# Eight attention jobs with places of their own, v scaled by ScalarE, tails issued by ScalarE, and weights rounded one chunk at a time

## The chip, the cores and the metric

One core of a Trainium2 chip. Times are device microseconds (us) of one execution, medians of several. All runs compared here are beside runs of the kernel before on the same chip.

## The reference, cut to what matters

```python
B, H, S, D = 8, 8, 576, 64
scores = 1/sqrt(D) * q @ k.T
Dmat[h, i, j] = gamma[h] ** (i - j) if i >= j else 0     # retention: decay per head
attn = (scores * Dmat) @ v                               # (B, H, S, D)
x = attn.transpose(0, 2, 1, 3).reshape(4608, 512)        # tokens x d_model
xn = x / sqrt(mean(x * x) + 1e-6) * rms_g
out = (silu(xn @ w_gate) * (xn @ w_val)) @ w_out         # d_ff = 1536; the weights are float64
```

The kernel splits the attention into 32 *jobs* of two heads. The float64 weights come in 18 *chunks* of 1 MB, which are rounded to float32 on chip: an *exponent* step (one VectorE operation, then three on ScalarE), a *mantissa* of three VectorE operations, and a *join* (one). Before the first projection can run, eight jobs must be done and the first two chunks rounded. This beginning is all that the change touches.

## The kernel before

A job's transposes; each result goes to a PSUM bank of a pool of five, and ScalarE copies it out. `last` of `turn` holds the tails (the last 64 rows of q and k):

```python
    def turn(j):
        d = st[j]
        hp = jobs[j][1]
        last = bank(f"turn_{j}_t")
        for nm in "qk":
            ps = bank(f"turn_{j}_{nm}")
            ...                                    # TensorE: four blocks of q or k into ps
            nc.scalar.copy(out=t[:, : NFULL * P], in_=ps)
        for i, nm in enumerate("qk"):
            ...                                    # TensorE: the tail into last[:, o]
            nc.scalar.copy(out=d[nm + "T"][:, NFULL * P :], in_=last[:, o])
        for e in range(2):                         # scale v by the decay, on GpSimd
            for t in (d["v"][:, :, e], d["vt"][:, e].unsqueeze(1)):
                g = gv[: t.shape[0], hp, e : e + 1].unsqueeze(2).to_broadcast(list(t.shape))
                nc.gpsimd.tensor_tensor(out=t, in0=t, in1=g, op=ALU.mult)
```

The states of a job (TensorE) end in a bank of the same pool, `d["last"] = bank(f"last_{j}")`; VectorE reads it in the last of the job's running sums. The order of the rounding, and the beginning:

```python
    def rounding():
        exponent(0); yield
        exponent(1); yield
        yield from mantissa(0); yield
        for i in range(len(chunks)):
            if i + 1 < len(chunks):
                yield from mantissa(i + 1); yield
            join(i)
            n_chunks += 1
            load_chunks(i + 4)
            yield
            if i + 2 < len(chunks):
                exponent(i + 2); yield
    ...
        load_first(0); load_tails(0); load_first(1); load_first(2)       # all by the sync queue
        load_chunks(1, nc.sync)
        for i in (1, 0, 2, 3):
            table(i)                                                     # issued by ScalarE
        nc.scalar.dma_start(out=rms_g, in_=...)
        turn(0)
        for j in range(8):
            slot(j)                         # values of j-1, scores, states, sums of j, carried of j-1
            if j + 1 < 8:
                turn(j + 1)
            ...                             # part of the norm of unit 0
            if 1 <= j <= 5:
                load_first(j + 2)           # waits for a buffer of k and v
            if j == 1:
                load_tails(1)
            ...
            load_chunks((1, 2, 2, 3, 3, 4, 4, 4)[j], nc.sync)
            weights((0, 1, 2, 2, 2, 2, 1, 0)[j])                         # rounding steps
```

## Time and profile before

| kernel before | |
|---|---|
| time | 1186.49 us, median of 3 (1185.11 to 1187.63) |
| span of the profiled run | 1186.8 us (one more execution, of 1188.96 us) |
| TensorE, VectorE, ScalarE, GpSimd busy | 97%, 57%, 20%, 5% (62.0 us) |
| rounds of the first eight jobs | 8.63, 5.77, 6.23, 6.61, 11.79, 10.07, 8.38, 7.95 us |
| first up matmul; start of its steady stretch | 69.37; 90.35 us |

A *round* runs from one job's first transposing matmul to the next job's. From 90.35 us on TensorE hardly waits, so a kernel is faster by as much as that point comes earlier, if the rest keeps its length. The profile counts an engine's wait before the instruction that ended it and names a releaser; "issue" means that the profile shows nothing it waited for.

### The profile page before, as it was taken

The page shows a single profiled execution, that of the slowest core. Times are in us where ns is not written, and L with a number is a line of the kernel's source. Part 1 is how long each engine was busy: PE and PEld are TensorE (multiplying, and loading weights), DVE is VectorE, ACT ScalarE, POOL GpSimd, SP SyncE. Part 2 cuts the span into 40 slices and gives each one's busy share as a digit, 9 for nine tenths or more (in the row PEclk, how much of TensorE's full clock was granted, in tenths as well). Part 3 has the DMA queues.
Part 4 walks back from the last instruction along what each step waited for, and adds up shares of the span by engine and source line. Part 5 has one row for each costly group of instructions (what it writes and reads, how often), then busy time and mean ns, then how long its engine had stood idle before and what let it go on. Part 6 is the DMA issues. An engine that isn't in the chain of part 4 may idle for free.

```text
span 1186.8 us, 24268 instructions
## 1 busy us (share of the span) xinstructions
PE 1147.7 (97%) x10320; PEld 1039.1 (88%) x10320; DVE 672.2 (57%) x1362; ACT 238.9 (20%) x452; POOL 62.0 (5%) x106
## 2 busy tenths in 40 slices
PE   7679999999999999999999999999999999999998
PEld 6555555448999999999999999999999999999998
DVE  4678785027765674464675666356566555536442
ACT  4325653012111120121120211220220110120110
POOL 2300004420000000000000000000000000000000
PEclk9799999999999999999999999999999999999999
DMA  8724431422755546315525456306435412403304
GB/s 223 180 63 142 146 138 36 137 66 49 203 149 87 131 121 116 110 44 103 146 61 119 100 132 130 123 2 133 101 98 127 118 49 83 131 1 93 121 1 107
DMA packets 282219, 125.23 MB, mean 106 GB/s; under 512 B 257152, under 2 KB 264704, under 8 KB 282112
## 3 DMA queue, kind: packets, MB, share of 16 engines
q1 hardware_dynamic: 271824, 108.44, 36.9%
q10 hardware_dynamic: 10288, 15.25, 4.1%
q8 instruction: 81, 1.33, 0.5%
q14 instruction: 26, 0.21, 0.1%
HBM read 108.70 MB, written 14.94 MB: 104 GB/s over the span
## 4 chain that ended last, share of the span: by engine, by line
PE 78%; DVE 11%; ACT 5%; DMA 3%; issue 2%; SPq 1%; POOL 0%; DVEq 0%; POOLq 0%; ACTq 0%
PE x L456 13%; PE z L456 13%; PE w L456 13%; PE wo L586 7%; PE y L456 6%; PE out L527 5%; PE xo L586 4%; PE zo L586 4%; PE yo L586 3%; PE up L513 2%; DVE sum L298 2%; PE av L334 2%; ACT w_gate L708 1%; ACT w_gate L709 1%; ACT w_gate L712 1%
## 5 line engine op out<-in xcount | busy, mean ns | idle before, releaser
L480 ACT COPY m<-x 128x384 f32<-128x384 f32 x60 | 28.7, 478 | 429.7 <-PE x L456 429.7
L456 PE MATMUL z<-x,w_gate 128*128 128x192 f32 x480 | 88.2, 327 | 2.2 <-DVE sum L298 2.2
L456 PE MATMUL x<-x,w_gate 128*128 128x192 f32 x480 | 89.8, 331 | 0.0
L456 PE MATMUL x<-x,w_val 128*128 128x192 f32 x480 | 88.7, 328 | 0.0
L456 PE MATMUL w<-sums,w_gate 128*128 128x192 f32 x480 | 88.0, 327 | 0.0
L456 PE MATMUL z<-x,w_val 128*128 128x192 f32 x480 | 87.8, 326 | 0.0
L456 PE MATMUL w<-sums,w_val 128*128 128x192 f32 x480 | 87.8, 326 | 0.0
L586 PE MATMUL xo<-h,w_out 128*128 128x192 f32 x480 | 82.1, 328 | 0.0
L586 PE MATMUL wo<-h,w_out 128*128 128x192 f32 x480 | 82.0, 328 | 0.0
L456 PEld LDWEIGHTS z<-x,w_gate 128*128 128x128 f32 x480 | 79.6, 190 | 2.5 <-DVE sum L298 2.5
L456 PEld LDWEIGHTS x<-x,w_gate 128*128 128x128 f32 x480 | 80.5, 192 | 0.5
L456 PEld LDWEIGHTS w<-sums,w_gate 128*128 128x128 f32 x480 | 80.0, 191 | 0.0
L456 PEld LDWEIGHTS x<-x,w_val 128*128 128x128 f32 x480 | 79.2, 190 | 0.6
L456 PEld LDWEIGHTS w<-sums,w_val 128*128 128x128 f32 x480 | 79.7, 190 | 0.0
L456 PEld LDWEIGHTS z<-x,w_val 128*128 128x128 f32 x480 | 79.6, 190 | 0.0
L586 PEld LDWEIGHTS xo<-h,w_out 128*128 128x128 f32 x480 | 78.1, 190 | 0.5
L586 PEld LDWEIGHTS wo<-h,w_out 128*128 128x128 f32 x480 | 78.1, 190 | 0.0
L463 DVE TENSOR_TENSOR u<-m,y 128x384 f32<-128x384 f32 x60 | 32.8, 546 | 78.0 <-PE y L456 75.6
L463 DVE TENSOR_TENSOR h<-u,w 128x384 f32<-128x384 f32 x60 | 33.2, 554 | 75.0 <-PE w L456 75.0
L513 PE MATMUL up<-x,w_gate 128*128 128x384 f32 x192 | 65.2, 498 | 4.9 <-DVE w_gate L742 3.1
L475 ACT ACTIVATE h<-h 128x384 f32<-128x384 f32 x90 | 47.0, 523 | 88.8 <-DVE h L463 88.8
L513 PE MATMUL up<-x,w_val 128*128 128x384 f32 x192 | 62.7, 487 | 1.7 <-ACT w_val L521 1.7
(124 smaller groups left out, 1756.8 us busy)
## 6 DMA issues: line engine op xcount, KB each, us to landing
w_out<-w_blocks SPq DMA_DIRECT2D x70, 768.0 KB, 5.3
k<-in_k_dram SPq DMA_DIRECT2D x64, 128.0 KB, 3.1
v<-in_v_dram SPq DMA_DIRECT2D x64, 128.0 KB, 3.8
out_dram<-o SPq DMA_DIRECT2D x304, 24.0 KB, 1.6
qraw<-in_q_dram SPq DMA_DIRECT2D x96, 72.0 KB, 2.7
kraw<-in_k_dram SPq DMA_DIRECT2D x96, 72.0 KB, 2.8
w_blocks<-w_out SPq DMA_DIRECT2D x7, 768.0 KB, 6.9
w_out<-in_moe_w_gate_dram ACTq DMA_DIRECT2D x4, 1024.0 KB, 5.2
```

Source lines behind the costliest of these rows:

```text
L298: nc.vector.scalar_tensor_tensor(out=t[:, c], in0=t[:, c - 1], scalar=gc[:, hp : hp + 1], in1=part, op0=ALU.mult, op1=ALU.add,)
L334: mm = nc.tensor.matmul(av[odd][side(e), i * L : i * L + L], lhsT=d["sum"][side(e), c - 1], rhs=d["qT"][side(e), c * L : c * L + L], start ...
L456: nc.tensor.matmul(ps[:, i * HU : i * HU + HU], lhsT=w_up[m][:, 2 * blk + c, cut], rhs=t_of[u][blk][:, c], start=(start and i == c == 0), ...
L463: nc.vector.tensor_tensor(out=o, in0=a, in1=pairs_of(ps), op=ALU.add)
L475: nc.scalar.activation(out=o, in_=c, func=AF.Silu)
L480: nc.scalar.copy(out=s1, in_=pairs_of(x_))
L513: nc.tensor.matmul(ps[:, :U], lhsT=w_up[m][:, 4 * half + c, i * P : i * P + P], rhs=x_of[u][:, c], start=(c == 0), stop=(c == NHP - 1),)
L527: nc.tensor.matmul(ps[:, :DM], lhsT=h_of[u][:, f, s * P : s * P + P], rhs=w_out[:, f], start=(f == 0), stop=(f == NF - 1),)
L586: nc.tensor.matmul(ps[:, i * HU : i * HU + HU], lhsT=w_slots[:, k % 4, c, i * P : i * P + P], rhs=rhs[:, c], start=(start and i == c == 0) ...
L708: nc.scalar.activation(out=e.bitcast(F32), in_=e, func=AF.Relu, bias=least)
L709: nc.scalar.activation(out=e.bitcast(F32), in_=e.bitcast(F32), func=AF.Relu, bias=most, scale=-1.0)
L712: nc.scalar.activation(out=e, in_=e.bitcast(F32), func=AF.Relu, bias=top, scale=-(2.0**23))
```

## The change

Its intent is to take waits out of the beginning. k and v of all eight jobs get places that nothing else uses by then, so that the sync queue can issue all loads at once; ScalarE scales v, as it does in all later jobs, so that GpSimd does not disturb VectorE; the first tails are issued by ScalarE, beside the sync queue; and a chunk is finished before the next one's mantissa starts.

```diff
+    def find_places():            # k: the 7 buffers of k and v, and qraw; v: sums, t1, unused weight room, h
+        ...
     def load_first(j):
...
-        load_kv(j, tail=False)
+        for nm, src in (("k", k), ("v", v)):
+            t = d[nm] = first_places[nm][j].rearrange("p (c e d) -> p c e d", e=2, d=D)
+            ...                   # the same two loads each, into the place
     def turn(j):
...
-        for e in range(2):
-            for t in (d["v"][:, :, e], d["vt"][:, e].unsqueeze(1)):
-                ...
-                nc.gpsimd.tensor_tensor(out=t, in0=t, in1=g, op=ALU.mult)
     def rounding():
         exponent(0)
         yield
-        exponent(1)
-        yield
-        yield from mantissa(0)
-        yield
         for i in range(len(chunks)):
-            if i + 1 < len(chunks):
-                yield from mantissa(i + 1)
-                yield
+            for ahead in (True, False):
+                if i + 1 in words_of and i + 1 not in exp_of and (i > 1 or not ahead):
+                    exponent(i + 1)
+                    yield
+                if ahead:
+                    yield from mantissa(i)
+                    load_chunks(i + 5)
+                    yield
             join(i)
             n_chunks += 1
-            load_chunks(i + 4)
             yield
-            if i + 2 < len(chunks):
-                exponent(i + 2)
-                yield
...
-        load_first(0)
-        load_tails(0)
-        load_first(1)
-        load_first(2)
-        load_chunks(1, nc.sync)
+        first_places.update(find_places())
+        load_tails(0, nc.scalar)
         for i in (1, 0, 2, 3):
             table(i)
         nc.scalar.dma_start(out=rms_g, in_=moe_rms_g.rearrange("(c p) -> p c", p=P))
+        for j in range(2 * NHP):
+            load_first(j)
+            if j == 3:
+                load_tails(1, nc.sync)
+            load_chunks((0, 0, 1, 1, 2, 2, 2, 3)[j], nc.sync)
+        load_chunks(4, nc.sync)
         turn(0)
+        scale_v(0)
         for j in range(2 * NHP):
             slot(j)
             if j + 1 < 2 * NHP:
                 turn(j + 1)
+                scale_v(j + 1)
...
-            if 1 <= j <= 5:
-                load_first(j + 2)
...
-            load_chunks((1, 2, 2, 3, 3, 4, 4, 4)[j], nc.sync)
-            weights((0, 1, 2, 2, 2, 2, 1, 0)[j])
+            weights((0, 1, 2, 2, 2, 2, 0, 0)[j])
```

More of the change, by code (lines that the diff above doesn't have):

```diff
@@ L128 @@
     st = [{} for _ in jobs]
-    x_of, t_of, h_of = {}, {}, {}
+    x_of, t_of, h_of, first_places = {}, {}, {}, {}
     def load_qk(j):
@@ L148, in load_first @@
         b, hp = jobs[j]
-        part = h_of[0].rearrange("p f t -> p (f t)")[:, j * 4 * P : j * 4 * P + 4 * P]
-        st[j]["q"] = part.rearrange("p (e t d) -> p e t d", e=2, d=D)
+        d = st[j]
+        room = h_of[0].rearrange("p f t -> p (f t)")
+        part = room[:, j * 4 * P : j * 4 * P + 4 * P]
+        d["q"] = part.rearrange("p (e t d) -> p e t d", e=2, d=D)
         nc.sync.dma_start(
@@ L154, in load_first, with load_tails @@
         )
-        load_kv(j, tail=False)
-    def load_tails(b):
+        for nm, src in (("k", k), ("v", v)):
+            t = d[nm] = first_places[nm][j].rearrange("p (c e d) -> p c e d", e=2, d=D)
+            for e in range(2):
+                nc.sync.dma_start(
+                    out=t[:, :, e],
+                    in_=src[b, 2 * hp + e, : NFULL * P].rearrange("(c p) d -> p c d", p=P),
+                )
+    def find_places():
+        n = NFULL * 2 * D
+        kv = {
+            nm: [raw.tile([P, n], F32, tag=nm, name=f"first_{nm}_{i}", bufs=bufs) for i in range(bufs)]
+            for nm, bufs in (("k", 4), ("v", 3))
+        }
+        other = raw.tile([P, S], F32, tag="qraw", name="first_k_7")[:, :n]
+        sums = [ffn.tile([P, 3 * 2 * HU], F32, tag=t, name=f"first_{t}") for t in ("sums", "t1")]
+        room = h_of[0].rearrange("p f t -> p (f t)")[:, 2 * NHP * 4 * P :]
+        more = w_up[1][:, 8:].rearrange("p b f -> p (b f)")[:, 6 * DM :]
+        return {
+            "k": kv["k"] + kv["v"] + [other],
+            "v": [t[:, i * n : i * n + n] for t in sums for i in range(2)]
+            + [more[:, i * n : i * n + n] for i in range(3)] + [room],
+        }
+    def load_tails(b, queue):
         room = w_up[1][:, 8:].rearrange("p b f -> p (b f)")
@@ L163, in load_tails, with load_kv @@
             t = t.rearrange("p (h d) -> p h d", d=D)
-            nc.sync.dma_start(out=t, in_=src[b, :, NFULL * P :].rearrange("h p d -> p h d"))
+            queue.dma_start(out=t, in_=src[b, :, NFULL * P :].rearrange("h p d -> p h d"))
             for hp in range(NHP):
                 st[b * NHP + hp][nm] = t[:, 2 * hp : 2 * hp + 2]
-    def load_kv(j, tail=True):
+    def load_kv(j):
         b, hp = jobs[j]
@@ L178, in load_kv @@
             st[j][nm] = t
-        if not tail:
-            return
         t = st[j]["vt"] = raw.tile([L, 2, D], F32, tag="vt", name=f"vt_{j}", bufs=3)
@@ L188, in turn @@
         d = st[j]
-        hp = jobs[j][1]
         last = bank(f"turn_{j}_t")
@@ L213, in turn @@
             nc.scalar.copy(out=d[nm + "T"][:, NFULL * P :], in_=last[:, o])
-        for e in range(2):
-            for t in (d["v"][:, :, e], d["vt"][:, e].unsqueeze(1)):
-                g = gv[: t.shape[0], hp, e : e + 1].unsqueeze(2).to_broadcast(list(t.shape))
-                nc.gpsimd.tensor_tensor(out=t, in0=t, in1=g, op=ALU.mult)
     def prepare(j):
@@ L822, in start @@
                 norm_0(0, [NHP - 1])
-            if 1 <= j <= 5:
-                load_first(j + 2)
-            if j == 1:
-                load_tails(1)
-            elif j == 5:
+            if j == 5:
                 norm_1(0)
-                load_qk(2 * NHP)
             elif j == 6:
                 norm_2(0)
-                load_kv(2 * NHP)
-            load_chunks((1, 2, 2, 3, 3, 4, 4, 4)[j], nc.sync)
-            weights((0, 1, 2, 2, 2, 2, 1, 0)[j])
+            weights((0, 1, 2, 2, 2, 2, 0, 0)[j])
+        load_qk(2 * NHP)
+        load_kv(2 * NHP)
         for m, g in [(m, g) for g in range(NG) for m in range(2)]:
```

## The prediction

> **What bounds the kernel now.** I read the 40 slices first. A slice is 29.7 us; columns 3 to 5 of the rows below show where anything can be won.
>
> ```profile
> PE   7679999999999999999999999999999999999998
> PEclk9799999999999999999999999999999999999999
> DMA  8724431422755546315525456306435412403304
> ```
>
> TensorE is at 90% or more from the fourth slice (89 us) to the end. The change touches nothing after about 205 us, so only the first three slices hold TensorE time to recover. A windows table whose stretches are the rounds of the first eight attention jobs (each from one job's first transposing matmul to the next job's; the last two are the entry into the up projection and the up projection itself) tells which rounds are long.
>
> ```profile
> 12.57:18.34 5.77, 5.18 (x165) 4.57 (x162) 3.79 (x13) 1.49 (x4) 2.67 (x8) 1.00 1.11 277
> 18.34:24.57 6.23, 5.20 (x166) 4.38 (x163) 4.47 (x17) 4.21 (x7) 2.36 (x6) 1.00 0.85 212
> 24.57:31.18 6.61, 4.93 (x165) 4.21 (x163) 4.51 (x16) 3.33 (x8) 0.51 (x3) 1.00 1.08 290
> 31.18:42.97 11.79, 5.52 (x163) 4.65 (x163) 10.32 (x26) 4.95 (x8) 5.62 (x9) 0.90 0.89 235
> 42.97:53.04 10.07, 8.78 (x163) 7.50 (x162) 5.68 (x15) 1.92 (x5) 2.99 (x5) 0.50 0.48 104
> 53.04:61.42 8.38, 7.81 (x171) 7.11 (x169) 5.48 (x16) 1.91 (x5) 2.55 (x6) 0.72 0.88 211
> 61.42:69.37 7.95, 6.00 (x168) 4.57 (x165) 7.57 (x21) 2.01 (x5) 0.09 (x1) 1.00 0.14 24
> 69.37:90.35 20.98, 16.13 (x108) 9.41 (x109) 13.18 (x33) 7.46 (x10) 0.95 (x2) 0.92 0.16 51
> 90.35:206.00 115.65, 113.93 (x353) 66.93 (x354) 85.11 (x100) 59.77 (x69) 10.55 (x8) 1.00 0.36 118
> ```
>
> After the span come length and busy time of PE, PEld, DVE, ACT and POOL, then clock, DMA share and GB/s. A round can take 5.8 to 6.2 us; three took 8 to 12. DMA is full (share 0.85 and more) until 43 us: the loads are bandwidth bound, not only held by buffers. The last row is TensorE bound: about 353 matmuls at 0.32 us, with one wait of 1.7 us. So what counts is when the steady stretch at 90.35 can begin. The chain of work in order of time names what made the long rounds:
>
> ```profile
> 12.24 5.12 DMA v<-in_v_dram
> ...
> 23.39 6.83 DMA w_out<-in_moe_w_gate_dram
> 30.25 0.70 DVE w_gate L704
> 30.97 1.16 ACT w_gate L708
> 32.16 1.16 ACT w_gate L709
> 33.34 1.15 ACT w_gate L712
> ...
> 38.24 3.79 issue
> ```
>
> Round 31.18 is long because the second weight chunk's exponent was put into the DVE and ACT streams before the chunk had landed, and job 4's copies stood behind it; then TensorE stood 3.79 us with nothing visible to wait for. Its clock was 0.50 in the next round. At 69.37 the first up matmuls start, but TensorE waits 3.1 us for the second chunk's join, and x of unit 1 is ready only at 90.
>
> **What the Trainium skill says.** "SBUF — State Buffer", section "Who interferes with whom": GpSimd shares a port pair with VectorE; a VectorE instruction with two SBUF inputs contends with a GpSimd one that reads SBUF, and the later one blocks. The trace agrees: GpSimd's scaling of 64x64 takes 0.28 us alone and 1.27 us beside the rounding; VectorE's L734 took 1.88 us there and 1.22 us alone, the three diagonals of L412 1.73 us beside GpSimd and 0.68 us without. "TensorE: Matmul & The Clock Gate", Part 1: an idle window of about 3.4 us halves the clock until a busy one. The trace agrees: after the 3.79 us gap, 0.50 to 54 us. "DMA: Bandwidth & Descriptors", section "Issuing engines are not separate DMA queues": a second issuing engine saves issue time only. That bears on the tails. "Runtime: NRT & Kernel Launch", section "Instruction fetch mechanics": instructions come in 16 KiB blocks of 256, by DMA, and this is mostly hidden. The queue table has 81 instruction packets and 1.33 MB, which is 16 KB each; that the 3.79 us gap is such a fetch behind full DMA engines is my inference.
>
> **The change, part by part.**
>
> Own places: the sync queue no longer waits for jobs to release buffers (6.6 us in two waits, the longer 5.4 us before job 7's v). That buys little bandwidth: from 10 to 45 us the DMA moved 8.69 MB, 248 GB/s, at 96% share, and it will do so again. All q, k, v and tails of the eight jobs are 7.1 MB (24 loads of 256 KB and 6 of 128 KB), and chunks 0 and 1, which stand among them, 2.1 MB. With 1.5 MB by 10 us and 0.248 MB per us, job 7 is complete at about 10 + (9.2 - 1.5) / 0.248 = 41 us, at 45 us if chunk 4 (now issued in job 3's round by ScalarE) comes between. TensorE wants it at about 50. So data is ahead of compute from job 2 on. Chunk 0 lands near 18, chunk 1 near 30 us, ahead of their exponents at 21 and 37.
>
> Tails from ScalarE: in the kernel before, the first tails are issued from 5.4 us on and job 0's last copy waits for them until 10.3. Issued at about 1 us, they save some 2 us: job 0's states end at about 10.6 instead of 12.6.
>
> v on ScalarE: GpSimd loses 32 operations. ScalarE gains four per job; the same four later in this kernel span 193.15 to 194.53, so 1.4 us. They stand behind the job's four copies, and the state matmuls need them. In the round 12.57 the copies end at 15.95 (3.4 after the round starts) and states start at 16.75 (4.2). Now they start at 3.4 + 1.4 = 4.8, end at 5.4, and carried values end at 6.4 to 6.5. A quiet round thus grows from 5.8 to about 6.5 us. VectorE's part of a round is 4.7 us (two ret 0.9, eight sums 2.4, four x 0.95, sq 0.5), plus up to 2.3 us of rounding. It gains back about 2.5 us in all (1.4 of rounding, 1.05 of diagonals) as GpSimd leaves the port.
>
> One chunk at a time: nine rounding steps stand in the eight jobs (ten before), but they are other ones: exponent 0 (0.6 us on VectorE), mantissa 0 (0.6 + 1.15 + 1.15), exponent 1 (0.6), join 0 (1.15), mantissa 1 (2.9). At the entry into the up projection only join 1 is missing; before, all three of chunk 2's mantissa operations (2.97 us) stood ahead of it.
>
> Walking through: states end at 10.6, 17.1, 23.1 and, behind the 3.5 us of exponent 0 on ScalarE, 30.3 us; then 36.5 and, behind exponent 1, 44.1 us for job 5. VectorE: job 5's sums end at 47.4, x at 48.4, norm and diagonals at 50.2, last mantissa at 52.5. Job 6 could have its states at 50.6, so VectorE is the bound from here: sums of job 6 to 55.8, x and norm of unit 0 to 59.4, job 7's sums to 62.7. The first up matmuls start at 59.5 (69.37 before). Join 1 ends at 68.2 (80.9 before). Norm and x of unit 1: 6.5 us of VectorE after exponent 3 and a third of mantissa 2 give first x at about 76, against 90.35. Gain 14.4 us, if no stall of instruction fetch comes.
>
> After it TensorE is the bound as before: rounding steps per up group are the same two, 81 are left where 80 were. The load of chunk i+4 stands after mantissa i now, earlier than after the next join, so most waits for chunks on ScalarE vanish; exponents 15 and 16 get nearer to their loads and exponent 17 still waits for its own. I give this zero, perhaps +1 us.
>
> **The rivals.**
>
> (a) The fetch stall comes again. The TensorE program has the same 1,234 rows and DMA is as full at 37 us as it was, so the 3.79 us may recur in job 3's carried values. With a half clock after it, job 5's states slip from 44.1 to about 50, and as job 6 hangs on them, the whole gain falls by 7.7 us to about 6.5: time 1180. For it: the fetch queue is the same. Against it: the rounds before it lost only 0.5 us to such gaps. I give 40%.
>
> (b) ScalarE becomes the bound of the rounds: 3.8 us per job and 3.5 us where an exponent falls in. I have counted +0.7 and +1.7 us. If its waits pile up with those of TensorE, 7.5 us per round give 7 us less gain: 1179. For it: the states now wait for the last engine in the chain. Against it: its busy time is under 5.5 of 6.5 us on average.
>
> (c) The rounds were bandwidth bound and stay so. Job 7's data would then set the pace at 45 us, plus the 24 us that the walk has from job 7's transposes (52) to the steady start (76): 69, earlier than the VectorE path. So this does not bind, unless the DMA rate falls under 200 GB/s, as it did in single microseconds.
>
> (d) More gain: rounds stay at 5.8 us, the clock stays at 1.00, VectorE never waits. VectorE's work before the steady stretch is some 58 us after 12 us, so 70 us is a floor: gain 20 us, 1166. Faster by over 2% needs 23.7 us, below that floor.
>
> **Range and chances.** 14.4 us at 60% and 6.5 us at 40% give 11.3 us: 1186.5 - 11.3 = 1175 us. Low 1167 is floor (d) less a little; high 1182 is rival (a) with something of (b). Faster by over 2% 0.04, within 2% 0.95, slower 0.01.
>
> **What would show it.** Right: steady TensorE (no gap over 1 us) from 74 to 84 us; rounds of 6.3 to 7 us up to job 4; first up matmul at 59 to 65; GpSimd busy some 45 us instead of 62.0 (16 pairs of 0.6 + 0.28 us and their waits fall away); VectorE's L734 and L412 of the first 60 us at their undisturbed length; no wait of the sync queue for TensorE in the first 45 us; the stretch after the steady start still 115 to 117 us. Wrong: a gap marked "issue" of over 2 us and clock 0.50 around 40 us (rival a), rounds of 7.5 us with states waiting for ScalarE (b), copies or states waiting for a DMA (c), or a longer up stretch with TensorE waiting for a weight chunk, which I have put at no more than 1 us.

## The result, and the profile after

The kernel after took 1187.58 us (median of 4, 1186.54 to 1189.27) beside 1186.59 us of the kernel before on the same chip. The ratio is 1.0011, with a 95% interval of 0.9993 to 1.0028: no gain, where 11 us were predicted. The ratios are those of the fast runs of both kernels, and not quite the ratios of the medians.

The busy line and three rows of the 40 slices of the kernel after:

```profile
PE 1147.1 (97%) x10320; PEld 1039.0 (88%) x10320; DVE 670.8 (57%) x1362; ACT 248.1 (21%) x484; POOL 45.0 (4%) x74
...
PE   6789999999999999999999999999999999999998
PEclk9889999999999999999999999999999999999999
DMA  9734421422655546315525456305345412403304
```

GpSimd (POOL) fell to 45.0 us as foreseen, but TensorE's first slice went from 7 to 6 and its third from 7 to 8: time lost first, then won back in part. The windows table of the kernel after by rounds (columns as in the prediction: span, length, busy time of PE, PEld, DVE, ACT and POOL, granted clock, DMA share, GB/s):

```profile
3.92:15.65 11.73, 6.11 (x94) 4.93 (x94) 0.00 (x0) 2.68 (x8) 0.00 (x0) 1.00 1.11 208
15.65:23.93 8.28, 7.79 (x165) 6.75 (x163) 3.86 (x13) 2.78 (x8) 0.09 (x1) 1.00 0.92 259
23.93:29.62 5.69, 5.12 (x165) 4.38 (x162) 4.41 (x17) 4.12 (x10) 0.27 (x1) 1.00 0.89 192
...
62.37:74.38 12.01, 8.62 (x168) 6.82 (x165) 9.34 (x26) 3.19 (x9) 0.09 (x1) 0.72 0.31 95
74.38:91.13 16.75, 14.21 (x110) 8.58 (x109) 11.30 (x28) 9.29 (x12) 0.94 (x2) 1.00 0.34 65
91.13:207.38 116.25, 114.03 (x353) 67.03 (x354) 87.31 (x101) 57.73 (x67) 11.79 (x9) 1.00 0.32 109
```

Round 0 takes 11.73 us instead of 8.63, the second 8.28 instead of 5.77, and the last 12.01 instead of 7.95. The five rounds between take 38.44 us together instead of 43.08, and the entry into the up projection is 16.75 us instead of 20.98, but all this only makes good the loss: the steady stretch starts at 91.13 (before: 90.35). It is 0.6 us longer, which is in the bounds given. So the question is what lengthened the first two rounds and the last one, and why the middle gave no more. What TensorE waited for until about 90 us in the kernel after, the rows that matter here (total, times, longest):

```profile
PE turn_t L231 <- ACT qT L235: 7.6, 8, 4.1
PE turn_t L231 <- DVE sum L315: 4.0, 2, 3.1
PE av L351 <- issue: 1.7, 1, 1.7
PE s L290 <- issue: 1.3, 1, 1.3
PE up L530 <- DVE w_gate L759: 0.8, 1, 0.8
```

In the kernel before these waits read:

```profile
PE av L334 <- issue: 3.8, 1, 3.8
PE up L513 <- DVE w_gate L742: 3.1, 1, 3.1
...
PE turn_t L209 <- ACT qT L213: 2.2, 5, 0.6
...
PE turn_t L209 <- DVE sum L298: 0.8, 2, 0.4
```

The gap marked "issue" and the wait for the second chunk's join shrank (3.8 to 1.7 and 1.3; 3.1 to 0.8). In their place stand two others: a wait of 4.1 us for ScalarE's copies at the start, and one of 3.1 us in the last round, in which a transpose of a tail waits for a *sum* of VectorE, that is, for data it does not use.

**The start.** ScalarE's timeline in the kernel after; ACTq rows are transfers that ScalarE issues, in its own order:

```profile
5.16 0.60 ACTq L189 DMA_DIRECT2D w_val<-in_v_dram  x1
7.59 0.44 ACTq L815 DMA_DIRECT2D gv<-gv_table  x1
...
9.04 0.33 ACTq L815 DMA_DIRECT2D gc<-gc_table  x1
...
11.15 0.45 ACTq L824 DMA_DIRECT2D rms_g<-in_moe_rms_g_dram  x1
11.65 0.58 ACT L228 COPY qT<-turn_q 128x512 f32<-128x512 f32 x1 [9.43 <-DMA gc<-gc_table]
```

The first copy in the kernel before:

```profile
5.95 0.58 ACT L206 COPY qT<-turn_q 128x512 f32<-128x512 f32 x1 [3.73 <-PE turn_q L201]
```

Eight transfers instead of five stand ahead of ScalarE's first copy. They take no more than 0.74 us each to issue, but from the third on there are pauses between them: in the built program both queues share eight completion semaphores, and a transfer waits until the earlier one that used its semaphore has landed. From the third transfer on, ScalarE's wait on the semaphores of job 0's and job 1's loads, of 128 and 256 KB, and of one of its own tails. The first copy starts at 11.65 instead of 5.95, and the states of job 0 end at 15.7 instead of 12.6.

The second round is longer for another reason: TensorE itself was slow. It was busy 7.79 us with 165 matmuls there, and 5.12 us with 165 in the next round; the four transposes of job 1's k took 1.12 us (before: 0.66). The clock column shows 1.00 in all of these, but the first clock record of the trace comes only at 23.0 us (before: 13.4). That this follows from the late start is not shown: x2, x8 and x15 below have second rounds of 8.28, 8.26 and 8.16 us after first rounds of only 9.1 to 9.4 us.

**The last round.** The transposes of the tails of job 7, after and then before (TensorE's timeline):

```profile
67.13 0.28 PE L231 MATMUL turn_t<-ident,w_val 64*128 64x64 f32 x1 [3.08 <-DVE sum L315]
```

```profile
63.25 0.27 PE L209 MATMUL turn_t<-ident,w_val 64*128 64x64 f32 x1 [0.15 <-ACT qT L206]
```

The banks of the two built programs explain the releaser. The pool has five banks, and which one a tile gets depends on what was released last at that point of the program; the new places of the rounding steps and of ScalarE's work changed that order:

| bank of | last_6 (read by job 6's last sum) | turn_7_q | turn_7_t |
|---|---|---|---|
| before | 4 | 7 | 7 |
| after | 4 | 3 | 4 |

After, job 7's tails go into the bank of job 6's last state and must wait for VectorE's last sum of job 6. Before, they went into the bank that q of the same job had just left.

### The profile page after: what moved, and what is told of

It reads as the page before. It is cut to its first block, busy times and chain, and to the rows that moved or that the text cites. A ratio compares the mean times of both kernels' runs of the same rounds, so it can differ in the third digit from the quotient of the medians.

```text
span 1184.7 us, 24258 instructions
## 1 busy us (share of the span) xinstructions
PE 1147.1 (97%) x10320; PEld 1039.0 (88%) x10320; DVE 670.8 (57%) x1362; ACT 248.1 (21%) x484; POOL 45.0 (4%) x74
## 4 chain that ended last, share of the span: by engine, by line
PE 85%; DVE 9%; ACT 2%; DMA 2%; issue 1%; SPq 0%; POOL 0%; DVEq 0%; POOLq 0%; ACTq 0%
PE x L473 13%; PE z L473 13%; PE w L473 13%; PE up L530 7%; PE wo L603 7%; PE y L473 6%; PE out L544 5%; PE xo L603 4%; PE zo L603 4%; PE yo L603 3%; PE av L351 2%; DVE sum L315 2%; PE av L332 1%; PE s L270 1%; PE s L290 1%; DVE sq L412 1%
```

## The experiments

Sixteen kernels ran (none is called x14). The median of "before" was between 1186.8 and 1188.3 us on all their chips. The later expectations call two things by short names: the *q bank* puts the tails into the PSUM tile of q, which takes the wait for `last_6` away; *later chunks* means that weight chunks 2 to 5 are loaded in job 6's round and not earlier.

| kernel | time, us (median, range, runs) | ratio to before (95%) |
|---|---|---|
| after | 1187.58 (1186.54 to 1189.27, 4) | 1.0011 (0.9993, 1.0028) |
| x1: after, tails by sync queue | 1182.48 (1179.52 to 1184.58, 6) | 0.9955 (0.9934, 0.9977) |
| x2: x1, v by GpSimd | 1184.09 (1178.99 to 1186.09, 6) | 0.9961 (0.9936, 0.9987) |
| x3: before, new rounding order | 1187.48 (1180.06 to 1188.51, 6) | 0.9988 (0.9959, 1.0016) |
| x4: before, own places | 1187.53 (1186.16 to 1188.92, 6) | 1.0000 (0.998, 1.002) |
| x5: x1, q bank | 1179.71 (1178.28 to 1182.46, 6) | 0.9942 (0.9927, 0.9956) |
| x6: x3, q bank | 1183.27 (1182.80 to 1184.48, 5) | 0.9973 (0.9959, 0.9986) |
| x7: after, few transfers on ScalarE | 1186.90 (1186.74 to 1187.66, 5) | 1.0001 (0.9989, 1.0013) |
| x8: before, v by ScalarE | 1186.13 (1184.19 to 1186.69, 5) | 0.9991 (0.9978, 1.0003) |
| x9: x5, later chunks | 1179.14 (1177.80 to 1180.83, 6) | 0.9930 (0.9914, 0.9945) |
| x10: x5, rounding steps earlier | 1186.11 (1185.92 to 1189.45, 6) | 0.9991 (0.9976, 1.0006) |
| x11: x9 and x10 | 1179.38 (1178.70 to 1180.16, 5) | 0.9931 (0.9916, 0.9946) |
| x12: after, q bank | 1187.70 (1187.14 to 1188.44, 5) | 1.0000 (0.9986, 1.0015) |
| x13: x12, later chunks | 1181.17 (1180.96 to 1182.04, 5) | 0.9949 (0.9936, 0.9962) |
| x15: x6, later chunks | 1178.57 (1178.01 to 1181.66, 5) | 0.9931 (0.9918, 0.9945) |
| x16: x9, v by GpSimd | 1179.48 (1175.70 to 1180.88, 6) | 0.9928 (0.9913, 0.9943) |
| x17: before, later chunks | 1185.30 (1183.64 to 1186.38, 6) | 0.9982 (0.9967, 0.9996) |

### The parts of the change: x1 to x4, x8

x1 undoes the issue by ScalarE alone:

```diff
-        load_tails(0, nc.scalar)
...
             load_first(j)
+            if j == 0:
+                load_tails(0, nc.sync)
```

> The changed kernel, with the first tails issued by the sync queue again, right after job 0's loads. Theory A (the loss sits in ScalarE's stream: with eight transfers in front of its first copy, each waiting for a transfer eight places earlier, that copy comes at 11.65 us instead of 5.95): the first copy is back near 6 us, the second round starts near 12.5 us instead of 15.65, TensorE reaches full clock near 14 us instead of 24, and the time falls by 4 to 7 us to 1180-1184. Rival B (what counts is ScalarE's scaling of v and the fetch stalls later; the early loss is absorbed by waits that come anyway): the first copy is back near 6 us, but the time stays within 2 us of the changed kernel (1186-1188).

It took 1182.48 us, some 5 us less than after. The states of job 0 are back (the second round starts at 12.79), and the steady stretch starts at 86.89. So in this kernel the issue by ScalarE cost 5 us, all that the change would have gained; the wait in the last round is unchanged (3.09 us).

x2 is x1 with `scale_v` of the eight jobs replaced by the kernel before's GpSimd loop:

> As the run before, and v of the first eight jobs scaled by GpSimd again. Theory A: scaling by ScalarE costs at most 0.7 us a round where ScalarE also has an exponent; against that stand VectorE's 2.5 us of interference; so within 2 us of the run before. Rival B (ScalarE in the chain is what ate the gain): faster than the run before by 4 us or more, rounds of 5.8 to 6.2 us.

The interval of x2 covers x1's ratio. x8 is the other way round, the kernel before with `scale_v(j)` in place of the GpSimd loop:

> The kernel before with v of the first eight jobs scaled by ScalarE in place of GpSimd, nothing else. The prediction's terms: quiet rounds 0.7 us longer, VectorE up to 2.5 us quicker; so within 1.5 us of before. Rival (b) of the prediction, ScalarE becomes the bound of the rounds: 3 us or more slower than before.

The interval of x8 just covers 1. Who scales v is worth nothing measurable here, although VectorE's three diagonals do fall to 0.68 us: TensorE hardly waited for VectorE's sums in the first 92 us of the kernel before (1.0 and 0.8 us in all).

x3 is the kernel before with the `rounding` part of the diff alone and its row of steps:

> The kernel before, with the new order of rounding and its earlier loads alone. If the new order is worth what the prediction put on it (the entry into the up projection loses the 2.97 us of chunk 2's mantissa and exponent 1 no longer stands before job 4's work): 3 to 6 us faster than before, 1181-1183. If the exponents and mantissas only move into other rounds and hold TensorE's transposes there instead: within 1.5 us of before.

x4 is x2 with the old `rounding` and its row of steps, so that own places and early loads remain alone:

> The kernel before, with places of their own for k and v and all loads issued up front, tails by the sync queue, v scaled by GpSimd, old order of rounding. Prediction's view (bandwidth bound, but data ahead of compute from job 2 on, exponent 1 no longer waits for its chunk, job 7 not for a buffer): 3 to 8 us faster than before. Rival (loads were never what bound it; the round with the fetch stall at half clock returns): within 1.5 us of before.

Both are as fast as before. For x4 that is the answer: own places are worth nothing. The prediction's reason, that the DMA engines were full anyway, was not tested alone. x3's one run of 1180.06 against a median of 1187.48, and waits of 4.14 and 2.14 us for the sum in its profile, said that something eats what the new order gives.

### The bank: x5, x6, x12

```diff
         d = st[j]
-        last = bank(f"turn_{j}_t")
         for nm in "qk":
             ps = bank(f"turn_{j}_{nm}")
+            if nm == "q":
+                last = ps
```

> The first run of this series (changed kernel, first tails by the sync queue), with job tails transposed into the PSUM bank of the same job's q, after its copy, in place of a bank of their own. Theory C: with the new order of rounding the build gives job 7's tail transposes the bank that job 6's last state sum is read from, so they wait for VectorE (3.09 us in that run, and a half clock after it; 0.75 us more in job 5). Without it the last round of the attention falls from 12.0 to about 8 us and the time by 3 to 5 us to 1178-1180. Rival: VectorE bounds that round anyway (diagonals, two mantissa operations, sums of job 6 and norm of unit 0 stand in a row there); then the wait moves to another place and the time stays within 1.5 us of 1182.5.

> The kernel before with the new order of rounding alone, which gained nothing (4.14 us of wait for VectorE's sums in job 7's tails, 2.14 us in job 5's), now with the tails in q's bank. Theory C: 3 to 5 us faster than before, 1182-1184. Rival (VectorE's order bounds that stretch): within 1.5 us of before.

x5 gains 2.8 us on x1 and x6 4.2 us on x3 (medians), and the tails' wait for the sum is gone in x5 and 0.4 us in x6; the last round of x5 is 7.46 us (x1: 11.96). So the bank is the cause of that wait. What it is worth in time is less sure: the ranges of x5 and x1 overlap, x3 has one run below all of x6, and the intervals of the ratios overlap in both pairs. The new order with its bank mended is worth 3 us over before. The same edit in the kernel after:

> The changed kernel as it is, tails still by ScalarE, with the tails' transposes in q's bank. If the two losses (ScalarE's stream at the start, the shared PSUM bank at the end) are independent, this takes away the second alone: 2.5 to 5 us faster than the changed kernel, 1182.5-1185. If the late wait only absorbed what the start lost: no change, 1187.

It gained nothing. The wait for the sum is gone here as well and the last round is 6.66 us, but x12 stands with "issue" for 2.03 us in job 3's carried values and for 4.04 us in job 5's states, the round with the second gap takes 12.37 us and the next one 10.36. Half the clock was granted for 13.7 us from 54.4 on. One loss was exchanged for another.

### ScalarE's transfers again: x7

If the number of transfers ahead of the first copy is the cause, it helps to keep the tails on ScalarE and take the other tables from it:

```diff
-        load_tails(0, nc.scalar)
-        for i in (1, 0, 2, 3):
-            table(i)
-        nc.scalar.dma_start(out=rms_g, ...)
+        table(1)
+        load_tails(0, nc.scalar)
...
+            if j == 1:                            # after the loads of job 1
+                for i in (0, 2, 3):
+                    table(i, nc.sync)
+                nc.sync.dma_start(out=rms_g, ...)
```

> The changed kernel with the first tails still issued by ScalarE, but with only the table for v and the tails in its stream; the other three tables and rms_g are issued by the sync queue after job 1's loads. Theory A (not the tails by ScalarE, but eight transfers ahead of ScalarE's first copy, the later ones waiting for others to land, hold it): the first copy comes before 8 us, and the time is that of the run with tails by the sync queue or better, 1180-1183. Rival (the tails' transfers themselves delay job 0's q, k or v by sharing the DMA engines): the first copy waits for TensorE beyond 8 us and the time stays above 1185.

The mechanism at the start is right: ScalarE's first copy is at 7.31 us in x7,

```profile
7.31 0.58 ACT L228 COPY qT<-turn_q 128x512 f32<-128x512 f32 x1 [5.09 <-DMA first_k<-in_k_dram]
```

and the second round starts at 13.79, not 15.65. (What is left of the delay is in part a wait of ScalarE for the tail of v, 2.25 us.) The time is not: 1186.90 us. Its TensorE stood 3.6 us with "issue" in job 5's states (after: 1.27) and had half a clock for 20.4 us of its first 120. Again a gain of 2 us early on was gone by 91 us.

### The gaps: x9 to x11, x13

TensorE's gaps marked "issue" come at the same few places of the program, above all in job 3's carried values and in job 5's states, with quite different lengths. If they are instruction fetches behind full DMA engines, as the prediction supposed, then job 5's must shrink when less is being loaded beside it. x9 moves chunks 2 to 5:

```diff
-                    load_chunks(i + 5)
+                    if i > 1:
+                        load_chunks(i + 5)
...
-            load_chunks((0, 0, 1, 1, 2, 2, 2, 3)[j], nc.sync)
-        load_chunks(4, nc.sync)
+            load_chunks((0, 0, 1, 1, 2, 2, 2, 2)[j], nc.sync)
...
                 norm_2(0)
+                load_chunks(6)                    # job 6's round
```

> The fastest run so far (tails by the sync queue, tails in q's bank, 1179.7), with weight chunks 2 to 5 loaded only in job 6's round, by ScalarE, so that no weight transfer runs beside the attention after about 42 us. Theory D (the gaps of TensorE marked issue, 0.93, 1.34 and 0.86 us there from 39 to 57 us and 2.37 at 33 us, are instruction fetches that queue behind full DMA engines): the gaps after 42 us fall under 0.5 us each and the time by 1 to 3 us. Rival (a fetch takes about as long whatever the DMA does, since the changed kernel has a gap of 1.27 us while its DMA share is near zero): gaps of 1 us and more remain at the same places, the time stays within 1 us.

x10 is x5 with the rounding steps taken earlier, which was to finish chunk 1 sooner, and x11 has both edits:

```diff
-            weights((0, 1, 2, 2, 2, 2, 0, 0)[j])
+            weights((0, 1, 3, 2, 3, 0, 0, 0)[j])
```

> The fastest run so far, with the nine rounding steps in the rounds of jobs 1 to 4 (1, 3, 2, 3) and none in job 5's, where norm and diagonals already keep VectorE. The prediction's claim that VectorE bounds from job 5 on: mantissa 1's 2.3 us leave that stretch, so 1.5 to 3 us faster, 1177-1178. Rival (TensorE's chain of copies, fetch gaps and clock bounds there too): within 1 us.

> Both of these. If both hold: the sum, 1174-1177. If neither does: 1179-1180.

x9 is within the noise of x5, whose gaps were short. x10 lost 6.4 us on x5, and x11, which differs from x10 in the chunk loads alone, got them back: 1186.11 against 1179.38 us. Beside x9 the earlier steps brought nothing (1179.38 against 1179.14), so that VectorE bounds from job 5 on, as the prediction had it, is not borne out. x10's trace is of its slowest execution (1189.45), but the steady stretch starts at 88.74 us in it and at 82.81 in that of x11, so most of the difference arises in the beginning. The windows table of x10 in steps of 1 us, where job 5's states stand (columns as above):

```profile
50.00:51.00 1.00, 0.00 (x0) 0.00 (x0) 0.98 (x2) 0.00 (x0) 0.00 (x0) 1.00 1.04 401
51.00:52.00 1.00, 0.00 (x0) 0.00 (x0) 0.99 (x1) 0.00 (x0) 0.00 (x0) 1.00 1.10 418
52.00:53.00 1.00, 0.00 (x0) 0.00 (x0) 1.00 (x2) 0.00 (x0) 0.00 (x0) 1.00 0.94 356
```

TensorE (the first pair) does nothing while DMA moves 356 to 418 GB/s at a share of about 1. It goes on at 54.23, after the transfers have ended at about 53.3, with the clock at half:

```profile
54.23 0.59 PE L291 MATMUL s<-w_val,first_v 64*64 64x64 f32 x12 [4.60 <-issue]
```

In x11 the DMA engines are idle at that time, and TensorE's work runs on:

```profile
50.00:51.00 1.00, 1.00 (x41) 1.00 (x34) 1.00 (x2) 0.00 (x0) 0.00 (x0) 1.00 0.08 16
```

Job 5's states over all kernels, with the DMA share during the gap:

| | gap in job 5's states, us (DMA share in it) |
|---|---|
| early chunks | x10 4.60 (0.82), x12 4.04 (0.53), x3 3.88 (0.88), x7 3.65 (1.01), x6 2.47 (0.85), x4 1.83 (0.00), x1 1.47 (0.85), x5 1.34 (0.41), x8 1.28 (0.51), after 1.27 (0.02), before 0.80 (0.43); in x2 none of 0.2 us or more |
| later chunks | x17 1.47 (0.52), x11 0.25 (0.00); in x9, x13, x15 and x16 none of 0.2 us or more |

Every gap of over 2 us here stands beside DMA engines that are at least half busy, and moving the chunks away brings it down to 1.5 us or less: loads beside it make it long, as x10 and x11 show by one edit. But a gap of 1.3 or 1.8 us comes beside idle engines too (after, x4), and x2 has early chunks and no gap.

Whether these are instruction fetches can be read from the traces, which hold the time of every DMA packet. The answer of `prof x10_steps_earlier --dma --window 51.7:51.8` shows one packet of the instruction queue starting within that tenth of a microsecond:

```profile
q8 instruction: 1, 0.02, 65.4%
```

| job 5's states | gap, us | packet of 16 KB, start to end |
|---|---|---|
| x10 | 49.63 to 54.23 | 51.73 to 52.78 |
| x12 | 50.95 to 54.99 | 52.60 to 53.65 |
| x4 | 48.71 to 50.54 | 47.96 to 49.32 |
| after | 51.68 to 52.95 | 50.56 to 51.65 |
| x11 | 49.17 to 49.42 | 47.09 to 48.01 |

It is the same everywhere: in the 18 traces TensorE has 47 gaps marked "issue" of 0.3 us or more up to 92 us, and every one ends 1.2 to 1.8 us after a packet of this queue has landed. Of its 232 other waits of that size, which have a named releaser, 28 do. So the gaps are instruction fetches, as far as traces can show it. The packet itself takes 1.05 us in x10 and 0.92 in x11; what differs is when it starts, 4.6 us later in x10 than in x11. In x4 and after it moved just as the loads were ending, before the gap, so the idle engines beside these gaps are no sign against the loads. When a fetch is asked for the trace does not show, and no run changed the fetches themselves: that the packets queue behind the loads stays an inference.

x13 puts the same two repairs into the kernel after, tails still with ScalarE:

> The changed kernel with the tails in q's bank (1187.7, as before), and with weight chunks 2 to 5 loaded in job 6's round. Theory D (a fetch behind full DMA engines gives back what the other waits lose): the gap of 4.04 us in job 5's states falls under 0.5 us, the half clock of 13.7 us after it goes with it, and the time falls by 4 to 7 us to 1181-1184. Rival (the start by ScalarE alone keeps it at 1187): within 1.5 us of 1187.7.

1181.17 us, 6.5 us less than x12. Against x9, 2.0 us slower, it differs in the tails alone. With the gaps out of the way this is what their issue by ScalarE costs, if anything: the two intervals overlap. The 5 us between x1 and after had more in it.

### How little of the change is needed: x15 to x17

x15 is x6 with later chunks, so the kernel before with new rounding order, q bank and later chunks; v is scaled by GpSimd, and the old places and load order stay:

> The kernel before with the new order of rounding and tails in q's bank (1183.3), and weight chunks 2 to 5 later. Theory D: its gap of 2.47 us in job 5's states falls under 0.5 us and the time by 1.5 to 4 us to 1179.5-1182. But its k and v still wait for buffers, which may set the pace of jobs 5 to 7; if that is what bounds it, no change (1183).

1178.57 us: as fast as x9. x16 takes v back to GpSimd in x9:

> The run with later chunks and tails by the sync queue (1179.1), with v of the first jobs scaled by GpSimd again. Prediction's terms: scaling by ScalarE lengthens quiet rounds by 0.7 us but frees VectorE of 2.5 us: within 1.5 us either way. If ScalarE's place in the chain costs more, 3 us or more faster than 1179.1; if GpSimd's interference with VectorE costs more, 3 us or more slower.

1179.48 us, no difference. x16 differs from x15 (1178.57) in the own places and the early loads alone, so these bring nothing here either, with the other losses gone. Last, later chunks in the kernel before alone:

```diff
-            load_chunks(i + 4)
+            if i:
+                load_chunks(i + 4)
...
-            load_chunks((1, 2, 2, 3, 3, 4, 4, 4)[j], nc.sync)
-            weights((0, 1, 2, 2, 2, 2, 1, 0)[j])
+            load_chunks((1, 2, 2, 2, 2, 2, 2, 2)[j], nc.sync)
+            if j == 6:
+                load_chunks(6)
+            weights((0, 1, 2, 2, 2, 2, 0, 0)[j])
```

> The kernel before, with one edit: the weight chunks 2 to 5 are loaded in job 6's round by ScalarE, not from job 1 on; the old order of rounding, the old places and the old banks stay. Theory: the later chunks alone take away the fetch gap beside full DMA, and with it the half clock after it (13.7 us of half clock follow the 38-us gap of the kernel before), so it is 2 to 5 us faster, ratio 0.996 to 0.998. Rival: the kernel before's last rounds are held by the wait of 3.12 us for the rounding of w_gate and by its buffers, whatever the clock; then it is within 1.5 us of before (ratio 0.999 to 1.001), and the gain of the fastest version needs the new rounding order with the later chunks.

1185.30 us, ratio 0.9982: 2 us, the lower edge of the theory. No gap marked "issue" is over 1.7 us now and the first up matmul comes at 65.73, 3.6 us earlier; but TensorE then waits 5.6 us, where it waited 3.1, for the second chunk's join. VectorE's timeline in x17, up to that join:

```profile
72.81 0.69 DVE L704 TENSOR_SCALAR w_gate<-w_out 128x1024 uint32<-128x1024 uint32 x1
...
77.08 1.23 DVE L734 SCALAR_TENSOR_TENSOR w_gate<-w_out,w_gate 128x1024 uint32<-128x1024 uint32 x1 [1.72 <-ACT w_gate L712]
78.22 1.22 DVE L742 SCALAR_TENSOR_TENSOR w_gate<-w_gate 128x1024 f32<-128x1024 f32 x1
```

In the old order exponent and mantissa of the next chunk (L704 to L734) stand ahead of the join (L742). This is what the new order takes away: later chunks alone bring 2 us, the new order with its bank 3 us, both 8 us (x15).

## Why the prediction was wrong

**The step that failed first: "Tails from ScalarE": "Issued at about 1 us, they save some 2 us: job 0's states end at about 10.6 instead of 12.6."** The first tail was issued at 0.93 us, but ScalarE's first copy went from 5.95 to 11.65 us and the states ended at 15.7. The working asked when the tails would land and not what stands behind their issue: ScalarE copies the transposes as well, in order, and its transfers wait for semaphores that the sync queue's new flood of loads holds. Turned round (x1), the change is 5 us faster than it was, of which at most 2.0 us remain once the other losses are gone (x13 against x9, overlapping intervals).

**The step that was missing: the banks.** "Walking through" counts engines and data, and takes it that TensorE's transposes need only q, k and a free engine. The new order gave job 7's tails the bank of job 6's last state: waits of 3.08 and 0.96 us, and a last round of 12.0 us. Taking them out was worth 2.8 us (x5) to 4.2 us (x6) by the medians, with ranges that overlap, and nothing while the tails stayed on ScalarE (x12).

**The rival (a), "the fetch stall comes again", came, but not where it was put.** The gap in job 3's carried values was 1.73 us instead of 3.79, and one of 1.27 us in job 5's states joined it. Both, and the half clock after them, are not a fixed cost of 7.7 us. Their length depends on what is being loaded when TensorE comes to these places, so they take back what another repair gains: x12 and x7 lost there all that they had won, and x10 more than that.

How the predicted 59.5 us for the first up matmul became 74.38, by these terms: 5.1 us from the states of job 0 (15.7 instead of 10.6); 4.0 us of waits for the sum; 3.0 us of the two gaps. The remaining 2.8 us are not measured apart. TensorE's slow stretches are larger than that: the second round kept it busy 2.7 us longer than the third with as many matmuls, and the clock was 0.75, 0.87 and 0.72 in the last three rounds. The terms overlap, so this is a tally and no proof. From there the walk was right: 16.75 us to the steady stretch (predicted 16.5), then 116.25 us (predicted 115 to 117).

**What held.** GpSimd 45.0 us busy (45 predicted); diagonals 0.68 us; the quiet round from 23.93 took 5.69 us, less than the 6.5 that were predicted, and scaling by ScalarE cost nothing in x8 and x16, so rival (b) was over-feared; the second chunk's join all but ready (0.78 us). Data came ahead of compute: rival (c) did not bind. Right facts on parts off the path brought no time: own places nothing (x4, and x16 beside x15), v on ScalarE nothing (x2, x8, x16). The one part that pays is the order of rounding, 3 us with the bank mended and 8 us with later chunks besides, and the walk had given it no sum of its own. That VectorE is the bound from job 6 on, on which the predicted 59.5 us rest, found no support (x11 beside x9).

Some slips of the prediction change nothing: its chances give 11.24 us and not 11.3, the "columns 3 to 5" of the slices should be the first three, and its "1,234 rows" stand in no view that was kept. The three diagonals read one tile and a column of scalars, so the rule of two inputs that it cites does not cover them; that they took 1.73 us beside GpSimd and 0.68 us without stands.

The fastest versions found, x15 (1178.57 us), x9 (1179.14), x11 and x16, beat both kernels by some 8 us, 0.7% of the time. They cannot be told apart.

## What to carry to other kernels

Before a transfer is moved to another engine's queue, look at what that engine computes next, and count the transfers ahead of it and what their semaphores wait for. When work is put in another order, compare which buffers the rotating tiles get: a wait for data that an instruction does not read can point to a shared bank. And if several sound repairs each bring nothing, look for a loss that grows when the others shrink, here TensorE's gaps beside full DMA engines, and remove that one together with each.

## What the Trainium skill lacked or had wrong

- "DMA: Bandwidth & Descriptors", section "Issuing engines are not separate DMA queues", says that a second issuing engine saves issue time only. It does not say what it can cost: ScalarE's eight issues of at most 0.74 us held its first copy until 11.65 us (before: 5.95), as six of them, in the built program, wait for a completion semaphore that an earlier transfer still holds. I found no page on what such waits cost.
- "Runtime: NRT & Kernel Launch", section "Instruction fetch mechanics", says that crossing a block boundary is mostly hidden. In the beginning of this kernel it was so for most, but not for all: some 200 packets of the instruction queue stand in the first 95 us of the 18 traces, and 47 gaps of TensorE marked "issue" end 1.2 to 1.8 us after one of them has landed. They are up to 4.60 us long beside full DMA engines (x10), 0.25 us at the same place when the loads were moved away (x11).
- No page that I found says that a wait can come from the build's choice of a PSUM bank for a rotating tile: 3.08 us in the kernel after for a sum that the transpose does not read, none with another bank (x5).
